# First transform stage of a long convolution: one full-height matmul on a 256-column block-diagonal table in place of two row tiles, under a new written-out order

## The chip, the core and the metric

The kernel runs on one core of a Trainium2 chip. A core has a matrix engine (TensorE, PE in the profile; its weight loads are listed as PEld), a vector engine (VectorE, DVE), an activation engine (ScalarE, ACT), a general one (GpSimd, POOL) and SyncE (SP), which here only issues DMAs. The engines run side by side, each through its own list of instructions, and wait for each other by semaphores. The metric is the device time of one execution in microseconds, the median of several runs.

## The reference, cut to what matters

The reference is one block of a network on 2048 tokens of 640 channels: an adaptive layer norm, a gated long convolution, another adaptive layer norm and a gated mixer.

```python
mod = (_silu(c) @ w_mod).reshape(1, 6, 1, -1)         # sa, ca, ga, sb, cb, gb
h = _layernorm(x) * (1 + ca) + sa
kv = short_conv4(A_k, shift_k) * A_v                  # 4 taps along the tokens
y = irfft(rfft(pad(kv)) * rfft(pad(ssm_k)))[:2048]    # causal convolution, length 4096
x = x + ga * h * (y + kv * ssm_D)
h = _layernorm(x) * (1 + cb) + sb
z = gelu(h @ w_in);  z1, z2 = halves(z);  z2 = _layernorm(z2)
out = x + gb * ((z1 * (w_sp @ z2 + b_sp)) @ w_out)
```

The convolution is computed by transforms written as matmuls. A sequence of 2048 tokens is cut in 16 pieces of 128, and a transform has two stages: stage 1 combines the 16 pieces of a channel, stage 2 works within the 128.

## The kernel before, in words

**Units.** The 640 channels are five units of 128. For each unit there is a filter transform (K, from ssm_k) and a data transform (U, from kv): ten stage-1 passes. An input tile X of a pass has the partitions (g, n), 8 channels by 16 pieces, and the free axes c (16 groups of 8 channels) and 128 tokens. So one slice X[:, c, :] holds the 16 pieces of 8 channels.

**Stage 1** (`stage1`, line 393). A pass has four steps (`s1`) of S1C = 4 slices c. In each step, for each slice, the lower and the upper 64 partitions are multiplied separately with a table of 128 columns, `F1flat[half]`: 32 frequencies j by 4 channels g, block-diagonal in g. These are two row tiles of TensorE, eight matmuls of 64 rows in a step. A step's result is 128 x 1024 fp32, two banks of PSUM (tag s1); in the first unit the two halves go to two single banks instead, tags pz and pu. A copy (`s1c`, on ACT, or on VectorE in some places) brings it to X1 in the order of frequencies.

**The table** (`f1_table`, line 283). VectorE makes angles (f1a) and a mask (f1g, `gmask`, from the bits of the partition number), ACT takes a cosine (f1c), VectorE multiplies (f1m).

**Stage 2** (`forward`, 8 items a pass): six matmuls of X1 with the sine tables M2, of 128 or 256 columns. For K, ACT copies the result (khc). For U, VectorE multiplies it with K's (prod, T at line 448), twelve matmuls with the tables G2 bring it back (inv), and a copy (zc) puts it in Z. Z is transposed by a DMA (zt) or, for the last unit, by TensorE (zfl); the last matmuls (y, yl) give y, which is multiplied with the normed and gated input gh.

**Beside it.** `short_conv`: taps on TensorE with diagonal weights dg, times V on VectorE (tv), written to memory (kvw) and read back as X of U. Layer norm statistics (ln1), the modulation vectors (modr, modc), the products ghm and sums res. Then the mixer: z in four groups of 512 tokens (zz and gelu), of which the first is transposed by TensorE and the others by DMA (turn), and the spatial matmul with the output projection (lines 912 to 940), which are scheduled apart.

**The order.** All but the last part is recorded as operations with their dependencies (class Plan), and then issued in one order written out by hand in the file: `ORDER` lists each operation with the engine that does it (P, A, D, G or S for SP). An engine works through its own operations strictly in that order. `FILLS` lists filler matmuls on the identity matrix, of 512 columns, which go to PSUM tag s1 and whose results nobody reads; they keep TensorE active.

Of the kernel before, what the change touches and what calls it, by code (L numbers as in the profile page):

```python
# [33 lines left out]
FILLS = (4, 4, 4, 2, 3, 1, 2, 4, 2, 1, 1, 3, 1, 2, )  # L34
# [5 lines left out]
D13 D95 D7 D9 D96 D97 D115 S14 D98 D109 A0 D110 A5 A4 A1 D103 A2 A3 G124 D8 A10 D116 A117 D104 A105 A106 A111 S77 D81  # L40
D11 P979 P980 P981 P982 P139 D6 A100 D12 P142 D144 A143 A140 D141 A99 G18 P983 P21 P19 A112 S78 D82 P145 P148 S16 D22
G101 S15 P25 G107 G108 G102 D20 S17 D26 P23 D24 P984 P130 G113 A118 D119 G120 S29 S467 A150 A147 A146 D131 A27 S28
A149 P151 A152 P155 A156 P133 S30 D134 P153 A154 A114 D121 P127 D31 A128 D471 P157 A158 D472 D473 P163 P985 P34 D35
A122 D123 G132 P165 A164 P161 A162 A166 S79 S80 P38 D39 P986 P167 D169 P170 P32 D33 A168 P136 A172 A171 G43 P176 D178
P173 D175 A174 G125 P36 D37 P159 A177 P179 S83 D85 D180 P987 P211 S468 A160 A137 S40 G129 P191 D192 A212 P988 P187
D188 S41 P213 A214 P181 D182 P203 G135 P217 A218 G138 P193 A194 P195 P215 A216 A475 A476 P189 D204 D196 D190 P183 S84
D184 G55 P199 D200 P205 A206 P44 S42 D474 D477 P185 A186 D478 D479 P223 A224 G480 P221 A222 S509 D45 P50 D51 P235 A236
P197 A198 P207 D208 P241 A242 P231 A232 P48 D49 P239 P46 A240 D481 D493 P225 A226 P237 A238 D47 P219 P510 A220 P512
A513 D497 S470 D486 A487 P243 D244 P201 A202 P255 P209 A494 S86 D88 P275 A276 P229 A230 D256 P251 P245 D488 D252 G67
P279 A210 A511 D498 A280 P247 D248 S469 S514 P227 A228 A246 D495 D496 P253 D254 P515 P267 D268 A499 D500 D516 S52 P277  # L50
P517 A278 A482 P257 D518 P233 A234 P263 D483 G558 D264 G614 P281 G616 A282 P249 S53 P58 G537 D484 A258 S87 P299 A300
P289 A290 P283 A284 P265 P303 A304 S54 P297 A298 P287 A288 D489 D485 D490 D59 P62 D63 P305 P271 D272 A306 A250 P60 D61
P301 A302 P293 A294 S519 P520 G491 P295 D521 G535 A296 D492 D505 A506 A266 P522 P307 A507 S89 D501 D502 A503 D308 G536
D91 G538 P273 S543 P315 D274 A508 P56 P269 D57 A270 A504 D523 G541 S65 P339 A340 P335 P309 A310 D316 P317 P259 D336
D260 P345 A346 P319 A318 P337 A338 P343 P285 G539 D540 D542 D320 A344 G556 D557 P544 D545 P261 A286 P331 D332 G593
G597 P341 A342 P291 A292 P321 P546 A262 D547 P351 P323 A352 G560 A322 S64 P72 P355 A356 P548 D324 P357 S66 D73 S90
P363 D549 A358 D651 A364 S92 D657 D561 P361 A362 G652 P550 D551 P327 D328 D94 P70 D71 P367 P347 A368 P68 P365 A366
G559 P311 D312 P325 P369 D618 D562 D563 G553 P74 S564 A348 P333 A370 A326 P371 A334 D69 D75 S76 S93 P403 P329 D372
A404 P565 D566 D599 P353 A354 A330 P379 D380 G595 P407 A408 P567 D568 P387 P313 P373 A314 G600 P349 A350 D388 A374
P569 D570 G554 P405 A406 P381 G598 D382 P571 D572 P359 G620 A360 P375 D376 P409 A410 G596 D583 P389 A390 P395 D396  # L60
P427 A428 D573 P411 A412 P377 P419 P399 D594 D587 D378 A420 G619 D400 P431 P397 D398 A432 P425 A426 P429 A430 P391
P401 D392 S601 P602 D603 A402 P383 P433 A434 P415 A416 D384 P604 D605 P393 A394 D586 P435 D436 P606 D607 P417 G658
P385 A418 G578 D582 P423 A386 A424 P451 D580 G617 P608 S698 P437 A438 D452 G552 D609 P421 A422 P443 D444 S524 P525
A526 G615 D655 P447 D448 P453 A454 P459 D460 P445 G613 A446 G656 G610 S622 G621 P455 D456 P449 A450 P463 D464 P461
A462 P413 A414 D574 P623 D624 P439 D440 D581 P457 G611 G588 S527 A458 P465 D577 A466 D653 P441 A442 P625 D576 P528
A529 S530 P663 A664 D612 D626 D579 D575 P627 D628 P659 D660 P989 P629 D630 P661 A662 P665 D666 D631 D632 D633 P990
P667 D668 D669 D672 D671 D670 P683 D700 D699 G654 G701 D684 P676 D677 D702 D703 D704 A126 P531 P690 D673 P533 A532
A534 P705 D706 P713 A714 D678 P711 D712 P991 P707 S697 D634 P709 D710 A708 P992 P741 D675 D635 D716 D674 P731 A742
G636 A732 D715 G717 D637 D638 D680 D782 D718 A719 D639 D720 P759 P738 P723 A724 D691 D685 P721 D679 A722 D781 A760
P734 P725 A726 P765 D681 D783 D640 D682 D784 G785 P727 D728 D786 D787 D789 D788 A735 P729 D641 D643 P763 D645 A730  # L70
D646 D642 G555 D688 A766 A790 P761 D585 P755 D592 A762 P773 A739 D649 A764 S791 D591 A756 D757 D647 P771 A772 P745
A746 D794 P767 A768 D793 D795 A774 P748 A749 P752 A796 P769 A770 A753 D792 P833 A834 D686 D589 P814 P825 A826 D644
D849 P797 A815 D590 P807 A808 D687 D848 D689 D584 D847 D850 G851 D852 D853 P821 D855 D854 A822 D692 D695 D816 D693
D696 D856 P800 A801 D694 D802 D915 A798 P827 A828 P811 D799 D648 D914 D747 D750 D751 D650 D916 A812 D813 D817 P831
A832 P804 A805 P837 A838 P818 A819 S857 D858 A862 D860 A861 P835 D913 P839 A840 P829 D859 P863 A830 G917 D806 A864
A836 D918 P884 D743 D809 P870 D919 D922 D920 A921 P901 A885 S923 A871 D872 D925 P895 A896 D926 P877 A902 P887 A888
D889 D928 P891 A892 D803 A878 D927 D736 P873 P866 A874 D875 A924 D754 A867 P899 A900 D740 D744 P880 A881 P929 P943
D758 A944 P932 A933 D820 A930 P893 A894 D823 D824 D810 G841 P946 A947 P936 A937 P959 D865 P961 P957 A960 A962 D842
D843 D845 A846 A844 P950 P967 D879 A968 D886 D733 D938 A951 P939 A940 D945 D868 P953 D737 D882 A954 G775 D776 A958
D890 A779 A778 P963 D869 D876 P905 D948 A964 D931 D883 G907 P903 A904 D908 D912 D934 D935 D949 A777 D911 P969 A906  # L80
P897 A898 D780 A910 D909 P965 D952 D955 D956 P971 A972 D941 D942 A970 G973 D974 A977 D975 D976 D978 A966
# [39 lines left out]
def kernel(  # L121
# [80 lines left out]
    with ExitStack() as actx:  # L202
# [3 lines left out]
        F1bd = consta.tile([P, NJ, 4], BF16)  # L206
# [16 lines left out]
        F1flat = F1bd[:].rearrange("p j g -> p (j g)")  # L223
# [27 lines left out]
        gmask, mpi, sgn = small("gmask", 4), small("mpi"), small("sgn")  # L251
        f1k, f1r, f1c = (consta.tile([P, NKC, 2], F32, name=n) for n in ("f1k", "f1r", "f1c"))
        f1i = consta.tile([P, NKC, 2], I32, name="f1i")
        bits = ((0, 15), (4, 3), (0, 3), (3, 15), (2, 1), (0, 1))
# [31 lines left out]
        def f1_table():  # L286
            def angles(e):
                e.scalar_tensor_tensor(f1i[:], f1k[:], pnum[:, 0:1], f1r[:], op0=ALU.mult, op1=ALU.add)
                e.tensor_scalar(f1i[:], f1i[:], 63, None, op0=ALU.bitwise_and)
            op("D", "f1a", angles, r=["bits0"], w=["f1a"])  # L290
            op("D", "f1g", lambda e: e.tensor_scalar(gmask[:], fidx[:, 0:4], pnum[:, 1:2], None, op0=ALU.is_equal),
               r=["bits0"], w=["f1g"])
            op("A", "f1c", lambda e: cosine(e, f1c[:], f1i[:]), r=["f1a", "sint"], w=["f1c"])
            op("D", "f1m", lambda e: e.tensor_tensor(
                F1bd[:], f1c[:].rearrange("p a b -> p (a b)")[:, :, None].to_broadcast([P, NJ, 4]),
                gmask[:, None, :].to_broadcast([P, NJ, 4]), op=ALU.mult), r=["f1c", "f1g"], w=["F1"])
# [96 lines left out]
        def stage1(u, X, X1):  # L393
            du = DU
            for ci, cp in enumerate(range(0, du // 8, S1C)):
# [5 lines left out]
                def mul(e, cp=cp, tiles=tiles, first=ci == 0):  # L401
                    if first:
                        new(X1, "X1", [P, NJ, DU])
                    ps = [new(*x, [P, 2 // len(tiles), S1C, NJ * 4], F32) for x in tiles]
                    for i in range(S1C):
                        for a in range(2):
                            half = slice(a * 64, a * 64 + 64)
                            mm((ps[a][:, 0] if pair else ps[0][:, a])[:, i, :], tl[X][half, cp + i, :], F1flat[half, :], True, True)

                def out_(e, cp, name, a0, na):  # L410
                    dst = tl[X1][:].rearrange("p j (a i g) -> p a j i g", a=2, g=4)[:, a0:a0 + na, :, cp:cp + S1C, :]
                    copy(e, dst, tl[name][:].rearrange("p a i (j g) -> p a j i g", g=4))
                op("P", "s1", mul, r=[(X, cp // 8 if pair else 0), "F1"] + ([(X1, "new")] if ci else []),
                   w=[x for x, _ in tiles] + ([] if ci else [(X1, "new")]), new=tiles + ([(X1, "X1")] if ci == 0 else []))
                na = 2 // len(tiles)
                for a, (x, _) in enumerate(tiles):
                    n1 = na * 128 * S1C
                    op("AD", "s1c", lambda e, cp=cp, x=x, a=a, na=na: out_(e, cp, x, a, na),
                       r=[x, (X1, "new")], w=[(X1, (cp, a))], n=n1)
# [567 lines left out]
```

## Time and profile before

| | |
|---|---|
| median of 13 runs | 339.95 us (338.14 to 342.63) |
| profiled execution | 340.28 us, its span 338.5 us |
| granted TensorE clock, mean | 0.99 |
| first matmul of stage 1 | 10.71 us |
| first matmul of the mixer | 149.24 us |
| busy: PE, DVE, ACT, POOL | 321.8, 219.6, 147.8, 72.0 us |
| stage-1 matmuls | 320 of 64 rows and 128 columns, in 40 steps |
| copies of 128 x 1024 after them on ACT | 32, mean 1.015 us |
| fillers | 34 matmuls of 512 columns |

The profile is one execution, seen by the hardware profiler. A line of a group or of the timeline names the line of the kernel, engine, operation, output and inputs, shapes, the count, the duration, and in brackets the idle time before it and what ended it. Line 237 is the helper of all matmuls in the first part and 240 that of all copies, so what they do is told by their tiles: s, pz and pu are PSUM tiles by tag, F1bd is the table of stage 1, X is the input or the result of stage 1, M and G are the sine tables, T is VectorE's product. Durations of TensorE overlap from one matmul to the next, so the cost of a group is taken from the start of the group to the start of the next.

### The profile page before, as it was taken

The numbers are of one execution on the slowest core, as the hardware profiler recorded it, in microseconds if no ns is written. First come the engines' busy times: TensorE is split into PE (matmuls) and PEld (weight loads), VectorE is DVE, ScalarE is ACT, GpSimd is POOL, SyncE is SP. The second block draws the span as 40 slices with busy tenths as digits, with TensorE's granted clock in tenths as the row PEclk, the third lists the DMA queues.
The fourth block names the chain that finished last, engine by engine and source line by source line (L and its number), as shares of the span: only waits on it lengthen the run. The fifth ranks groups of instructions, "written<-read, shape, count | busy, mean of one in ns | idle before, by whom it ended". The sixth has DMA issues, their size and how long they took to land.

```text
span 338.5 us, 6933 instructions
## 1 busy us (share of the span) xinstructions
PE 321.8 (95%) x2887; PEld 208.5 (62%) x2887; DVE 219.6 (65%) x460; ACT 147.8 (44%) x251; POOL 72.0 (21%) x88
## 2 busy tenths in 40 slices
PE   7789999998999899989999999999999999999995
PEld 2365868767768699845455555555555555555553
DVE  7699998989898999998685676253322232223323
ACT  2666889897667664538667579100000000000000
POOL 2561030568048606132001022000000000000000
PEclk9799999999999999979999999999999999999999
DMA  8989998999494938601442992165555566621421
GB/s 130 196 158 238 214 285 205 183 254 224 79 159 116 270 99 190 229 2 26 54 77 40 173 222 88 39 140 110 122 124 118 116 136 134 108 62 46 48 46 58
DMA packets 128582, 45.02 MB, mean 133 GB/s; under 512 B 117704, under 2 KB 127784, under 8 KB 128552
## 3 DMA queue, kind: packets, MB, share of 16 engines
q1 hardware_dynamic: 126448, 44.32, 62.5%
q10 hardware_dynamic: 2104, 0.27, 0.5%
q8 instruction: 22, 0.36, 0.4%
q14 instruction: 8, 0.07, 0.1%
HBM read 16.11 MB, written 5.24 MB: 63 GB/s over the span
## 4 chain that ended last, share of the span: by engine, by line
PE 53%; DMA 2%; DVE 1%; issue 0%; DVEq 0%
PE ps L919 28%; PE po L937 9%; PE pz L237 8%; PE pu L237 8%; DMA Z<-Z 2%; DVE Z L834 0%; PE sm L798 0%; PE s L237 0%; DVE u L922 0%; DVE ot L939 0%; DVE Z L807 0%; PE pt L929 0%; DVE Z L786 0%; DVE xt L661 0%; DVEq L834 0%
## 5 line engine op out<-in xcount | busy, mean ns | idle before, releaser
L919 PE MATMUL ps<-X,wT 128*128 128x432 bf16 x512 | 95.7, 346 | 0.0
L919 PEld LDWEIGHTS <-wT 128*128 128x128 bf16 x512 | 50.1, 98 | 42.2
L930 ACT COPY uT<-pt 128x896 bf16<-128x896 bf16 x1 | 0.9, 906 | 117.0 <-PE pt L929 117.0
L448 DVE TENSOR_TENSOR T<-pu,KH 128x1024 bf16<-128x1024 f32 x40 | 48.3, 1217 | 3.4 <-PE pu L237 1.6
L237 PEld LDWEIGHTS <-Z 128*128 128x128 bf16 x320 | 31.4, 99 | 28.4 <-issue 1.1
L237 PE MATMUL pu<-X,M 128*128 128x128 bf16 (+1 forms) x480 | 45.8, 237 | 2.4 <-DVE T L448 2.3
L237 PE MATMUL pz<-T,G 128*128 128x128 bf16 (+1 forms) x480 | 41.5, 237 | 0.8 <-DVE T L448 0.8
L237 PEld LDWEIGHTS <-M 128*128 128x128 bf16 x480 | 35.7, 98 | 8.6 <-issue 3.4
L922 DVE SCALAR_TENSOR_TENSOR u<-ps,bcol,G 128x432 bf16<-128x432 f32 x18 | 12.0, 667 | 42.2 <-PE ps L919 42.2
L237 PEld LDWEIGHTS <-G 128*128 128x128 bf16 x480 | 34.8, 98 | 4.6 <-DVE T L448 1.0
L240 ACT CAST X<-s 128x1024 bf16<-128x1024 f32 x32 | 32.5, 1015 | 11.1 <-PE s L237 11.1
L237 PE MATMUL pz<-big,Z 128*128 128x432 bf16 x160 | 33.1, 352 | 0.0
L937 PE MATMUL po<-w_o,uT 128*128 128x320 bf16 (+1 forms) x224 | 32.8, 299 | 0.0
L237 PE MATMUL pu<-big,Z 128*128 128x432 bf16 x160 | 32.0, 346 | 0.5 <-DVE Z L834 0.5
L937 PEld LDWEIGHTS <-uT 128*128 128x128 bf16 (+1 forms) x224 | 21.8, 98 | 9.8
L922 DVE SCALAR_TENSOR_TENSOR u<-ps,bcol,M 128x432 bf16<-128x432 f32 x14 | 9.3, 667 | 28.3 <-PE ps L919 28.3
L240 ACT CAST KH<-pu 128x512 bf16<-128x512 f32 x40 | 23.1, 592 | 8.1 <-PE pu L237 7.9
L939 DVE TENSOR_TENSOR ot<-po,xt 128x320 bf16<-128x320 f32 x32 | 15.7, 491 | 13.4 <-PE po L937 13.4
L240 ACT CAST Z<-pz 128x512 bf16<-128x512 f32 x33 | 19.2, 589 | 8.9 <-PE pz L237 8.9
L237 PE MATMUL sm<-big,dg 128*128 128x512 bf16 (+1 forms) x80 | 21.2, 393 | 1.0 <-DVE dg L503 1.0
L624 POOL TENSOR_TENSOR gh<-gh,gsa_bf 128x512 bf16<-128x512 bf16 x14 | 16.7, 1205 | 18.5 <-DVE gh L624 16.7
L863 DVE BATCH_NORM_STATS2 stz<-X 128x6 f32<-128x432 bf16 x32 | 17.7, 586 | 1.6 <-ACT X L857 1.6
(139 smaller groups left out, 371.1 us busy)
## 6 DMA issues: line engine op xcount, KB each, us to landing
wm<-in_w_mod_dram SPq DMA_DIRECT2D x6, 800.0 KB, 5.7
xt<-in_A_q_dram SPq DMA_DIRECT2D x4, 640.0 KB, 5.8
out_dram<-ot SPq DMA_DIRECT2D x16, 160.0 KB, 2.4
big<-in_B_w_in_dram SPq DMA_DIRECT2D x2, 1080.0 KB, 7.2
X<-in_A_ssm_k_dram SPq DMA_DIRECT2D x4, 512.0 KB, 7.3
kv_scr<-big SPq DMA_DIRECT2D x4, 512.0 KB, 3.4
X<-kv_scr SPq DMA_DIRECT2D x4, 512.0 KB, 5.7
w_o<-in_B_w_out_dram SPq DMA_DIRECT2D x6, 160.0 KB, 2.9
```

What stands on the lines that cost most here:

```text
L237: nc.tensor.matmul(o, lhsT=w, rhs=x, start=start, stop=stop)
L240: (e.copy if e is nc.scalar else e.tensor_copy)(dst, src)
L448: e.tensor_tensor(T_[:], tl[pu][:, :, :, None, :].to_broadcast([P, KP, 2, 2, DU]), tl[KH][:, :, None, :, :].to_broadcast([P, KP, 2, 2, DU] ...
L624: lambda e, vec=vec, o=o: e.tensor_tensor(gvu, gvu, vec[:, None, d0:d0 + du].to_broadcast([P, TB, du]), op=o),
L863: op("D", "stz", lambda e, i=i, n=n, fc=fc: e.bn_stats(out=stz[:, n, fc, :], in_=tl[z2][:, i, fc * FC:(fc + 1) * FC]), r=[(z2, (i, fc))], ...
L919: nc.tensor.matmul(ps[:, :FC], lhsT=wTs[t][:, s_, :], rhs=tl["z2_%d" % (s_ // TB)][:, s_ % TB, fc * FC:(fc + 1) * FC], start=(s_ == 0), st ...
L922: nc.vector.scalar_tensor_tensor(u[:, sl], ps[:, :FC], bcol[:, t:t + 1], z1[t][:, sl], op0=ALU.add, op1=ALU.mult)
L930: nc.scalar.copy(uTs[t][:], pt[:])
L937: nc.tensor.matmul(ps[:, :HS], lhsT=uTs[t][:fsz[ft], ft, :], rhs=w_o[:fsz[ft], ft, h * HS:(h + 1) * HS], start=(ft == 0), stop=(ft == NFT ...
L939: nc.vector.tensor_tensor(ot[:, h * HS:(h + 1) * HS], ps[:, :HS], xt[:, t, h * HS:(h + 1) * HS], op=ALU.add)
```

## The change

The table gets twice the columns: for every partition now (a, j, g), with a the lower or upper half of the eight channels, and the mask has eight columns instead of four, compared with three bits of the partition number instead of two. So one matmul of 128 rows and 256 columns gives for a slice what the two half-height matmuls gave together. A step has four matmuls instead of eight. The result of a slice now lies together, (a, j, g), and a bank holds two slices of both halves instead of four slices of one half; the copy to X1 reads it accordingly. In the first unit the two single banks hold two slices each. The total of copied elements stays.

The small loads of c, D and the taps may be given to GpSimd too, but stand where they were, on ACT. The order of all operations is new, with other engines for some of them, and twelve fillers of together 22 matmuls instead of fourteen of 34.

```diff
-FILLS = (4, 4, 4, 2, 3, 1, 2, 4, 2, 1, 1, 3, 1, 2, )
+FILLS = (4, 4, 4, 1, 2, 1, 1, 1, 3, 1, 2, 2, )
 ORDER = """
-D13 D95 D7 D9 D96 D97 D115 S14 D98 D109 A0 D110 A5 A4 A1 D103 A2 A3 G124 D8 A10 D116 A117 D104 A105 A106 A111 S77 D81
-D11 P979 P980 P981 P982 P139 D6 A100 D12 P142 D144 A143 A140 D141 A99 G18 P983 P21 P19 A112 S78 D82 P145 P148 S16 D22
+D13 D95 D12 D96 S14 D97 D103 D109 D104 D110 A0 D115 A5 A4 A1 A2 A3 A111 D98 A99 D6 D18 P979 P980 P981 P19 S16 A112 P21
+D7 D8 D9 S77 D81 S78 A10 D11 G124 G125 D20 P139 A106 D82 D141 P142 A105 A140 A144 P982 P145 A146 D22 G31 D143 D116
...
-        F1bd = consta.tile([P, NJ, 4], BF16)
+        F1bd = consta.tile([P, 2, NJ, 4], BF16)
...
-        bits = ((0, 15), (4, 3), (0, 3), (3, 15), (2, 1), (0, 1))
+        bits = ((0, 15), (4, 7), (0, 3), (3, 15), (2, 1), (0, 1))
...
             op("D", "f1m", lambda e: e.tensor_tensor(
-                F1bd[:], f1c[:].rearrange("p a b -> p (a b)")[:, :, None].to_broadcast([P, NJ, 4]),
-                gmask[:, None, :].to_broadcast([P, NJ, 4]), op=ALU.mult), r=["f1c", "f1g"], w=["F1"])
+                F1bd[:], f1c[:].rearrange("p a b -> p (a b)")[:, None, :, None].to_broadcast([P, 2, NJ, 4]),
+                gmask[:].rearrange("p (a g) -> p a g", a=2)[:, :, None, :].to_broadcast([P, 2, NJ, 4]), op=ALU.mult), r=["f1c", "f1g"], w=["F1"])
...
-                    ps = [new(*x, [P, 2 // len(tiles), S1C, NJ * 4], F32) for x in tiles]
+                    k = S1C // len(tiles)
+                    ps = [new(*x, [P, k, 2 * NJ * 4], F32) for x in tiles]
                     for i in range(S1C):
-                        for a in range(2):
-                            half = slice(a * 64, a * 64 + 64)
-                            mm((ps[a][:, 0] if pair else ps[0][:, a])[:, i, :], tl[X][half, cp + i, :], F1flat[half, :], True, True)
+                        mm(ps[i // k][:, i % k, :], tl[X][:, cp + i, :], F1flat, True, True)
...
-                    dst = tl[X1][:].rearrange("p j (a i g) -> p a j i g", a=2, g=4)[:, a0:a0 + na, :, cp:cp + S1C, :]
-                    copy(e, dst, tl[name][:].rearrange("p a i (j g) -> p a j i g", g=4))
+                    dst = tl[X1][:].rearrange("p j (a i g) -> p a j i g", a=2, g=4)[:, :, :, i0:i0 + k, :]
+                    copy(e, dst, tl[name][:].rearrange("p i (a j g) -> p a j i g", a=2, g=4))
...
-        op("SA", "ldc", lambda e: e.dma_start(c_bf[:], c[0].rearrange("(t p) -> p t", p=P)), w=["c"])
+        op("SAG", "ldc", lambda e: e.dma_start(c_bf[:], c[0].rearrange("(t p) -> p t", p=P)), w=["c"])
```

In the new order, among other moves: the first two tap groups of the short convolution (P19, P21) stand ahead of the first stage-1 step (P139), and their diagonal weights are made by VectorE (D18) ahead of the table's angles; the first half of V (S16) is loaded ahead of the first X (S77, S78); both writes of the first kv are issued by SP; the two halves of w_in are loaded earlier, ahead of the last K input; the preload of the gelu table (A126) stands near the end.

## The prediction

> **What bounds the kernel now.** I read the page's busy line and slices first, then the stages, then TensorE's timeline at single transform steps. Busy time, and the slices of 8.5 us:
>
> ```profile
> PE 321.8 (95%) x2887; PEld 208.5 (62%) x2887; DVE 219.6 (65%) x460; ACT 147.8 (44%) x251; POOL 72.0 (21%) x88
> PE   7789999998999899989999999999999999999995
> DVE  7699998989898999998685676253322232223323
> PEclk9799999999999999979999999999999999999999
> ```
>
> TensorE is nearly always occupied; VectorE nearly as much in the first 18 slices, and not after. The clock row dips twice. By stages (time, then busy us of PE, PEld, DVE, ACT, POOL, then clock):
>
> ```profile
> 0.00:11.00 11.00, 6.39 (x25) 2.15 (x27) 7.40 (x31) 3.92 (x10) 2.22 (x15) 1.00 0.94 141
> 11.00:50.00 39.00, 37.32 (x417) 24.97 (x411) 34.45 (x65) 28.12 (x50) 14.87 (x17) 0.96 1.02 222
> 50.00:100.00 50.00, 48.28 (x621) 37.65 (x620) 46.01 (x79) 41.49 (x65) 21.68 (x19) 1.00 0.97 184
> 100.00:149.00 49.00, 44.84 (x769) 39.47 (x764) 46.10 (x73) 28.24 (x45) 22.78 (x21) 0.99 0.60 162
> ```
>
> The mixer starts at 149.24 us; from there PE is busy 185 of 189 us with work the diff doesn't edit. So the 149 us in front decide. There PE is busy 136.8 us, VectorE 134.0: PE bounds, with VectorE 3 us behind. The chain of waits reaches back only to 146 us and can't say what set the front.
>
> One transform step on PE (start, duration, work, count):
>
> ```profile
> 41.24 1.05 PE L237 MATMUL pz<-T,G 128*128 128x256 bf16 x12
> 42.12 1.05 PE L237 MATMUL pu<-X,M 128*128 128x256 bf16 x12
> 43.01 1.03 PE L237 MATMUL sm<-big,dg 128*128 128x512 bf16 x4
> ...
> 45.19 0.60 PE L237 MATMUL pu<-X,M 128*128 128x256 bf16 x6
> 45.73 0.40 PE L237 MATMUL s<-F1bd,X 64*128 64x128 bf16 x8
> 46.06 0.61 PE L237 MATMUL pu<-X,M 128*128 128x256 bf16 x6
> 46.51 0.81 PE L237 MATMUL sm<-big,dg 128*128 128x512 bf16 x3
> ```
>
> Durations overlap, so starts are subtracted. Twelve pu matmuls take 43.01 - 42.12 = 0.89 us, six therefore 0.445; ahead of a stage-1 step the six take 45.73 - 45.19 = 0.54. So 0.095 us is lost in entering. The eight half-height matmuls then take 46.06 - 45.73 = 0.33 although their four pairs run at 0.056 each (pairs start at 15.45, 15.50, 15.56, 15.62 in the first unit), 0.22 together: 0.10 is lost in leaving. A step alone costs 0.425, of which 0.195 is switching.
>
> The start, where PE waits for the table:
>
> ```profile
> 10.29 0.20 DVE L389 TENSOR_TENSOR X<-X,D_col 128x8 bf16<-128x8 bf16 x1 [1.57 <-issue]
> 10.37 0.29 DVE L294 TENSOR_TENSOR F1bd<-f1c,gmask 128x128 bf16<-128x128 f32 x1
> ...
> 10.71 0.21 PE L237 MATMUL pz<-F1bd,X 64*128 64x128 bf16 x1 [2.19 <-DVE F1bd L294]
> ...
> 11.42 1.46 PE L237 MATMUL s<-ident 128*128 128x512 bf16 x3
> ```
>
> Until 10.71 us PE has done only filler. That wait is followed by a window at half clock, 11.05 to 14.46 us.
>
> [...] 3.41 us windows at 0.5, one after the table wait, one at 147.58 to 151.0; 512-column matmuls start 0.425 us apart there, 0.216 elsewhere. [...]
>
> **The change, part by part.**
>
> 1. Stage-1 matmuls. 40 steps of eight 64-row, 128-column matmuls become four 128-row, 256-column ones. Price of a 256-column matmul: twelve pz (four of 256, eight of 128) take 42.12 - 41.24 = 0.88; eight of 128 at 0.056 are 0.448; so 0.108 each. New step: 4 x 0.108 = 0.432, total 17.3 us. Old: 40 x 0.224 = 9.0, plus switching. In the order the 40 steps stand in 36 separate groups, 36 x 0.195 = 7.0; total 16.0. **+1.3 us of PE.** [...]
>
> 2. Fillers: 34 matmuls become 22, 12 x 0.216 = 2.6 us of PE. They fill gaps in which PE has nothing ready, so leaving them out is no gain by itself: I count zero here. That the new order has fewer such gaps to fill is worth something, at most 2.6 us; see (8).
>
> 3. The start. The first two tap groups of the short convolution now precede the first stage-1 step. They need dg (now built by VectorE ahead of the F1 angles) and the first K half. VectorE runs three of the four turn and msub pairs first; by its old timeline that ends about 7.6 us, then the sk cast 0.1 and dg 0.6: ready about 8.4 us. The K half has landed by 5.3 (the D load, which waits for it, starts at 5.34). F1bd still waits for D_col, as before at 10.29; its multiply doubles to 256 elements, 0.29 to an estimated 0.4; f1c stands behind three sines of 0.4 and is ready about 9.8, hidden by D_col. X's loads move behind one V transpose on SP (2.48 us issue) and should land 2 to 3 us later, still about when D_col does. So eight taps of 0.216, **1.7 us of real work, are done in a gap where PE had nothing.** **-1.7 us.** If PE's work from 8.4 to 10.1 also keeps the clock up, another 0 to 1.7 is saved; I take 0[...].
>
> 4. Copies out of PSUM: ACT's 128x1024 at 1.01 us as before, but the four innermost steps now alternate between two banks. No row shows that[...]. ACT has 149 - 102 = 47 us idle in front, so I take 0 on the path.
>
> 5. Moves between engines ahead of the mixer, counted in the two orders: VectorE gets +3 xn (0.44 each by start differences), +1 s1c (1.2), +1 zc (0.61), +1 gcopy (0.65), +1 zk (0.6), +2 gneg[...], +2 ln2, less one ghm, msgn, res and yml: **+4.4 us of VectorE, -7 of ACT.** VectorE has 15 us idle in front, so nothing on the path by itself; it is the cover that rival R1 takes away.
>
> 6. DMA queues. kv0's second write and first write both go on SP (one was ACT's); V0 moves ahead of X; w_in's halves of 1080 KB move ahead of the fifth K load and the last two Z transposes. w_in was loaded at 112.8 and 137.0 and is needed after 148[...]. Behind it on SP stand XK4 and ZT1. Landing takes 7.2 for the one and 5.6 for the other, 12.8 if the second waits for the first; SP can issue both once U3's load is out, and by the order's PE work (summed from the starts) K4's first step comes 12 us after that. No wait there before; bound 0 to 2 us, I take 0.3.
>
> 7. The mixer's beginning. Before, the second token group's transpose was issued 10 us in and PE waited:
>
> ```profile
> 158.53 3.02 SPq L826 DMA_TRANSPOSE Z<-Z  x1
> ...
> 165.94 1.09 PE L237 MATMUL pu<-big,Z 128*128 128x432 bf16 x5 [0.51 <-DVE Z L834]
> ```
>
> In the new order the transpose is emitted 6.9 us of PE work after the first mixer matmul instead of 9.7, while that group's first matmul stays at 15.1. The wait of 0.7 us (the start is 0.68 late) should go: **-0.7.** What is late next is the z2 normalisation, which shows no wait. The gelu table load (1.28 us) is no longer preloaded, but falls between the last modulation and the first gelu, while PE has a filler and a matmul group of 0.9; four PSUM buffers cover the rest: 0.
>
> 8. Fewer gaps. I credit 0.8 of the 2.6 in (2), since most measured stalls (0.8 to 1.7 us at 78, 84, 115, 138, 145) were queueing that fillers don't mark.
>
> Sum: +1.3 - 1.7 + 0.3 - 0.7 - 0.8 = -1.6 us. The profiled execution took 340.28 us (span 338.5 and 1.8 around it): 338.7. The median of 13 is 0.33 lower: **338.3.**
>
> **Rivals.** (R1) *VectorE becomes the bound, slower.* Up to the first stage-1 step of the last unit's K transform, summed start differences give VectorE about 88 us against PE's 87, where before it was 82 against 87. Products release each inverse matmul. Against: after that point VectorE has less to do than before. It decides once VectorE's idle in front, 15 us less 4.4, is less than what its waits for PE use; those waits were 8 us (2.9, 1.9, 1.6, 0.6, 0.5 and 0.4 in the list of waits). If two thirds of 4.4 us turn into PE waits, +2.9: 338.3 + 2.9 = 341.2; all of it, 342.7.
>
> (R2) *The gain at the start is hidden.* Stage 2 needs the M2 sines, signs and negations; if they arrive as before (first pu<-X,M at 18.34), PE idles for the taps' 1.7 us there. Then 338.3 + 1.7 = 340.0. Against: the new order has all four sign ops on POOL and three sines ahead of f1c.
>
> (R3) *It works better.* The clock dip at 11 us goes (-1.7) and idle time shrinks by another 0.6: 336.0. For it: [...] the fewer fillers.
>
> (R4) *The change doesn't do what it says*: the 0.195 is no mode switch but part of any change of tile, and stays: +7, 345.3. Against: pz to pu at 42.12 shows no such loss.
>
> **Chances.** Sum above 0.43; R3 0.17; R2 0.19; R1 0.19; R4 0.02. A measurement can tell about 0.3%, 1.0 us, from no change. The main case and R3 are faster, R2 within, R1 and R4 slower: 0.60, 0.19, 0.21. Range: the main case alone 337.0 to 339.3; to leave out no more than 2 in 10 it takes in most of R3 and R1: 335.6 to 341.6.
>
> **What would show it.** Stage-1 steps of four matmuls at 0.43 with no 0.1 us ahead or behind; taps at about 8.5 us, before the first F1bd matmul near 10.8; first pu<-X,M near 16.5; mixer's first matmul at 148.0 to 148.6 and no wait at the first transposed group; VectorE 138 us busy in front. Wrong if the mixer begins after 149.2, or PE's waits for T (3.1 us before) exceed 5.

## The result, and the profile after

| | before | after |
|---|---|---|
| median | 340.25 us (338.07 to 342.63, 48 runs) | 336.89 us (336.62 to 337.36, 11 runs) |
| ratio of the two | | 0.991, 95% interval 0.9889 to 0.9931 |
| profiled execution, its span | 340.28, 338.5 us | 337.21, 335.3 us |
| first stage-1 matmul | 10.71 us | 11.81 us |
| first forward transform (pu<-X,M) | 18.34 us | 18.07 us |
| U0's first stage-1 step | 26.61 us | 25.52 us |
| first inverse transform (pz<-T,G) | 34.20 us | 31.25 us |
| mixer's first matmul | 149.24 us | 145.79 us |
| from there to the spatial matmul (ps) | 60.51 us | 60.81 us |

The change makes the kernel faster by 0.9%, 3.4 us; 338.3 was forecast. All of it is there when the mixer begins, and 2.95 of the 3.45 us already at the first inverse transform. Of these 2.95 about 0.9 is only moved: six pu matmuls and one stage-1 step that stood ahead of that point now stand behind it. The times of the table also contain the half-clock windows of the two profiled executions: at 11.05 to 14.46 and 147.58 to 151.0 us before, at 140.8 to 144.2 after.

The page of the changed kernel, busy line and slices:

```profile
PE 321.2 (96%) x2719; PEld 214.3 (64%) x2719; DVE 222.7 (66%) x468; ACT 140.3 (42%) x242; POOL 72.7 (22%) x89
PE   6799999999989999999999999999999999999995
DVE  7988999899999999997885775263222332223323
PEclk9999999999999999889999999999999999999999
```

TensorE's busy sum has not changed, though 160 of the 320 stage-1 matmuls and eight fillers are gone: the new matmuls have twice the columns. The clock's dip in the second slice is gone; one is left at 140.8 to 144.2 us. The same stages as before:

```profile
0.00:11.00 11.00, 7.44 (x20) 2.23 (x20) 8.62 (x31) 3.31 (x9) 3.54 (x16) 1.00 1.00 136
11.00:50.00 39.00, 36.50 (x358) 27.87 (x359) 36.00 (x75) 30.21 (x54) 11.74 (x14) 1.00 1.02 236
50.00:100.00 50.00, 48.28 (x560) 40.61 (x558) 46.97 (x77) 36.42 (x59) 26.89 (x24) 1.00 0.92 206
100.00:149.00 49.00, 47.89 (x729) 41.00 (x726) 46.87 (x79) 26.83 (x43) 20.92 (x21) 0.97 0.54 129
```

VectorE is busy 138.5 us in the first 149, 134.0 before; but 3.2 us of the mixer lie in these 149 us now. Up to the mixer's first matmul it is busy 135.3 us, 134.2 before. A transform step on TensorE (start, duration, work, count):

```profile
32.13 0.60 PE L237 MATMUL pu<-X,M 128*128 128x256 bf16 x6
32.57 0.60 PE L237 MATMUL s<-F1bd,X 128*128 128x256 bf16 x4
33.01 1.05 PE L237 MATMUL pz<-T,G 128*128 128x256 bf16 x12
```

Six pu take 0.44, four stage-1 matmuls 0.44, and nothing is lost at either end. The start, on TensorE:

```profile
8.55 1.90 PE L237 MATMUL sm<-big,dg 128*128 128x512 bf16 x8 [0.64 <-DVE dg L502]
11.81 0.38 PE L237 MATMUL pz<-F1bd,X 128*128 128x256 bf16 x2 [1.36 <-DVE F1bd L294]
...
17.41 0.61 PE L359 MATMUL sm<-ident,M 128*128 128x128 bf16 x8 [1.24 <-POOL M L342]
...
18.07 1.05 PE L237 MATMUL pu<-X,M 128*128 128x256 bf16 x12
...
25.52 0.39 PE L237 MATMUL pz<-F1bd,X 128*128 128x256 bf16 x2 [0.36 <-DMA X<-kv_scr]
...
31.25 1.04 PE L237 MATMUL pz<-T,G 128*128 128x256 bf16 x12
```

The taps run at 8.55 at full clock, but the table comes 1.1 us later than before, and a new wait for the M2 signs stands ahead of the first forward transform. Then the mixer's beginning, first TensorE, then GpSimd and VectorE on the way to the first of these waits:

```profile
149.70 0.40 PE L797 MATMUL sm<-ident,Z 128*128 128x128 bf16 x4 [0.72 <-DVE Z L785]
156.42 1.07 PE L237 MATMUL pz<-big,Z 128*128 128x432 bf16 x5 [0.51 <-ACT M L856]
```

```profile
147.16 1.16 POOL L660 TENSOR_TENSOR xt<-xt,gh 128x512 bf16<-128x512 bf16 x1
147.23 1.10 DVE L773 SCALAR_TENSOR_TENSOR nmr<-mv,rstd 128x2 f32<-128x2 f32 x1
```

The wait for the transposed group (0.51 before) is gone; two others took its place.

**The clock as a second measure.** A window of 3.41 us at half clock lowers a run's mean clock by about 1.7 / 338 = 0.005, so a run's mean clock tells roughly how many such windows it had (in the profiled executions two and 0.990 before, one and 0.995 after). Of 100 runs of the kernel before beside the experiments, 11 had a mean of 0.998 or more (median 338.62), 31 had 0.993 to 0.997 (340.13) and 58 had 0.991 or less (340.62). Of the changed kernel's twelve runs whose clock was recorded, eight had 0.998 or more (336.75) and four 0.993 to 0.997 (337.15). So with the clock up in both the difference is 1.9 us; the other 1.5 us of the 3.4 go with windows at half clock, which the changed kernel has less often.

### The profile page after: what moved, and what is told of

Its sections match the earlier page's. It is cut to its first block, busy times and chain, and to the rows that moved or that the text cites. A ratio compares the mean times of both kernels' runs of the same rounds, so it can differ in the third digit from the quotient of the medians.

```text
span 335.3 us, 6591 instructions
## 1 busy us (share of the span) xinstructions
PE 321.2 (96%) x2719; PEld 214.3 (64%) x2719; DVE 222.7 (66%) x468; ACT 140.3 (42%) x242; POOL 72.7 (22%) x89
## 4 chain that ended last, share of the span: by engine, by line
PE 73%; DVE 16%; DMA 5%; issue 2%; POOL 1%; ACT 0%; DVEq 0%; SPq 0%; ACTq 0%
PE ps L918 28%; PE pz L237 15%; PE pu L237 14%; PE po L936 9%; DVE T L447 5%; PE sm L237 5%; PE s L237 2%; DVE big L517 2%; DMA D_col<-in_A_ssm_D_dram 2%; DMA X<-kv_scr 1%; DMA big<-in_A_k_dram 1%; DVE X L240 1%; DVE gh L623 1%; DVE st L666 1%; POOL rstd L183 1%
## 5 line engine op out<-in xcount | busy, mean ns | idle before, releaser
L237 PEld LDWEIGHTS <-Z 128*128 128x128 bf16 x320 | 31.1, 98 | 27.7 <-issue 1.1
L237 PE MATMUL pu<-X,M 128*128 128x128 bf16 (+1 forms) x480 | 45.4, 237 | 0.8 <-DVE T L447 0.7
L237 PE MATMUL pz<-T,G 128*128 128x128 bf16 (+1 forms) x480 | 41.2, 237 | 0.7 <-DVE T L447 0.6
L237 PEld LDWEIGHTS <-M 128*128 128x128 bf16 x480 | 37.1, 98 | 6.3 <-issue 1.3
L237 PEld LDWEIGHTS <-G 128*128 128x128 bf16 x480 | 35.3, 98 | 3.6 <-DVE T L447 0.8
L240 ACT CAST X<-s 128x1024 bf16<-128x1024 f32 x31 | 31.5, 1015 | 11.2 <-PE s L237 11.0
L237 PE MATMUL pz<-big,Z 128*128 128x432 bf16 x160 | 32.3, 346 | 0.5 <-ACT M L856 0.5
L237 PE MATMUL pu<-big,Z 128*128 128x432 bf16 x160 | 32.5, 346 | 0.1
L237 PE MATMUL sm<-big,dg 128*128 128x512 bf16 (+1 forms) x80 | 20.4, 379 | 1.1 <-DVE dg L502 0.6
L623 POOL TENSOR_TENSOR gh<-gh,gca_bf 128x512 bf16<-128x512 bf16 x14 | 16.8, 1205 | 16.9 <-DVE gca_bf L610 12.9
```

The costliest lines, as they stand in the source:

```text
L237: nc.tensor.matmul(o, lhsT=w, rhs=x, start=start, stop=stop)
L240: (e.copy if e is nc.scalar else e.tensor_copy)(dst, src)
L623: lambda e, vec=vec, o=o: e.tensor_tensor(gvu, gvu, vec[:, None, d0:d0 + du].to_broadcast([P, TB, du]), op=o),
```

## Experiments

In kernels with another order the code lines are shifted by six (L231 for L237). Times are medians; the ratio is to the kernel before.

**1. Shape and order apart.** The change couples a new matmul shape with a new order. Shape alone:

```diff
 # the changed kernel
-ORDER, FILLS = new
+ORDER, FILLS = those of the kernel before
```

> The order and the fillers of before, with the full-height stage-1 matmuls and their table alone. Theory A (the gain is in the order[...]): +0 to +1.3 us on before, 340.2 to 341.6. Rival B (the shape is what gains[...]): 337 to 338.5, most of the way to the changed kernel.

Measured 341.55 us (14 runs), 1.0022 [1.0004, 1.0041]. The full-height matmuls cost 1.2 us, as the forecast's step 1 had it (1.3). They don't gain anything by themselves.

Order alone, with the old row tiles:

```diff
 # the kernel before
-ORDER, FILLS = old
+ORDER, FILLS = those of the changed kernel
```

> The changed kernel's order and fillers, with the two row tiles of before. Theory A: the whole gain of the order without the 1.3 us that the full height costs, 335.5 to 337.0. Rival B: 339 to 341. A third outcome, 337.0 to 338.5, would say that the order has absorbed the difference and the shape doesn't matter to the time.

Measured 337.60 us (6 runs), 0.9913 [0.9891, 0.9935]: 0.7 slower than the changed kernel, not 1.3 faster: the third outcome of the expectation. Its mixer begins 1.28 us earlier (144.51; about 0.4 of this is the half-clock window just ahead of the changed kernel's mixer: experiment 9's profiled run, without one at a mean clock of 1.000, has the first transpose there at 143.00, the changed kernel at 143.42), but the way from there to the spatial matmul takes 62.4 us instead of 60.8. So under the new order what TensorE saves in front comes back as waits in the mixer. The list of waits of this kernel from 143 to 207 us (what waited, for whom, us in total, times, longest):

```profile
PE sm L792 <- DVE Z L780: 0.9, 1, 0.9
PE pz L231 <- ACT M L851: 0.5, 1, 0.5
PE pu L231 <- ACT Z L826: 0.4, 2, 0.2
PE pu L231 <- DVE Z L828: 0.4, 1, 0.4
PE sm L792 <- DVE Z L801: 0.2, 1, 0.2
```

The changed kernel has only the first two of them, 0.7 and 0.5.

**2. Start and rest of the order apart**, both with full height, cut at the first inverse transform.

```diff
-ORDER = new
+ORDER = new up to the first inverse, then the old order of what is left
```

> Full height. Up to the first inverse matmul the changed kernel's order and fillers, all other operations after that in the order of before. Theory A1 (of the 3.45 us that the mixer starts earlier in the profiles, 2.95 are there when the first inverse matmul starts): 337.0 to 338.5. Rival A2 (the order gains all along the first 145 us, and the early lead would be lost in a wait later): 339.5 to 341.

```diff
-ORDER = new
+ORDER = old up to the first inverse, then the new order of what is left
```

> Full height. Up to the first inverse matmul the order and fillers of before, the rest in the changed kernel's order. A1: most of the gain is gone, 339.3 to 341.3. A2: most of it stays, 337.0 to 338.5.

New start: 337.96 us (6 runs), 0.9931 [0.9906, 0.9957]. Old start: 341.55 us (22 runs), 1.0034 [1.0013, 1.0055], a little above A1's range. The start carries the gain: 341.55 (all old) less 337.96 is 3.6 us. The new rest behind an old start is worth nothing in the medians, behind the new start another 1.1 us (337.96 to 336.89).

Windows at half clock are only a part of this. Behind the new rest the start is worth 4.7 us in the medians (341.55 to 336.89), and still 3.0 with runs of a mean clock of 0.998 or more alone (339.8, 8 runs; 336.75, 8). The profiled execution with the old start had no such window in its first 330 us (mean clock 0.998), and shows where these 3.0 come from:

```profile
10.68 0.38 PE L231 MATMUL pz<-F1bd,X 128*128 128x256 bf16 x2 [3.15 <-DVE F1bd L288]
...
17.19 1.05 PE L231 MATMUL pu<-X,M 128*128 128x256 bf16 x12
...
25.80 0.39 PE L231 MATMUL pz<-F1bd,X 128*128 128x256 bf16 x2 [0.27 <-DMA X<-kv_scr]
...
34.05 1.05 PE L231 MATMUL pz<-T,G 128*128 128x256 bf16 x12
```

The changed kernel has these at 11.81, 18.07, 25.52 and 31.25. So with the clock up the new start is 0.9 us later at the first forward transform, level at U0's first stage-1 step, where both wait for the kv that is read back (0.27 and 0.36), and 2.8 us ahead at the first inverse, 0.9 of them the moved work. From the first forward transform to the first inverse, TensorE spends 4.6 us on fillers and idling behind the old start and 1.8 behind the new one (16.86 us less 12.3 of work; 13.18 less 11.4; the work counted by the starts, with 0.88 for twelve pu, 0.44 for four stage-1 matmuls and for eight of the L353 or L359 kind, 0.216 for a tap).

**3. What in the start?** The first tap groups put back behind the first two stage-1 steps, as in the old order:

```diff
-... P19 S16 A112 P21 ... D20 P139 A106 D82 D141 P142 A105 A140 A144 P982 ...
+... S16 A112 ... P139 A106 D82 D141 P142 A105 A140 A144 P19 P21 D20 P982 ...
```

> The changed kernel with the first two tap groups put back behind the first two stage-1 steps on TensorE, and the first product of the taps (VectorE) with them. Nothing else is edited, the dg block stays early. Theory T (my step 3: 1.7 us of real work is done in a gap): the median rises by 1.2 to 1.9 us, to 338.1 to 338.8, and both the first kv write and U0's first stage-1 step come later by about as much. Rival R2 (the gain was hidden, since the first forward transform waits for the M2 signs at 17.41 anyway, with 1.24 us of idle before it): the first forward transform stays within 0.4 of 18.07 and the median within 0.4 of 336.9.

Measured 340.95 us (22 runs), 1.0007 [0.9988, 1.0026]: the whole gain is gone with the place of these eight matmuls, over twice what theory T expected. TensorE in it:

```profile
11.61 0.59 PE L231 MATMUL pz<-F1bd,X 128*128 128x256 bf16 x2 [3.86 <-DVE F1bd L288]
...
13.27 3.62 PE L231 MATMUL sm<-big,dg 128*128 128x512 bf16 x8
...
22.15 1.05 PE L231 MATMUL pu<-X,M 128*128 128x256 bf16 x12
```

The wait for the table is 3.86 us, and what follows until 17.5 runs at half clock (the clock row has 0.6 in the slice of 8.5 to 17.0 us): the taps take 3.62 us, 1.90 in the changed kernel. The first forward transform comes 4.1 us later, U0's first stage-1 step 4.2, the mixer 3.8. From the lengths of the matmuls in this stretch of 5.9 us (columns at half clock less columns at full clock) 2.9 us are lost there to the clock; if all of that reaches the end, the other 1.1 to 1.2 is the order. The split isn't exact: two of these runs had a mean clock of 0.995, and at 339.95 are still 2.8 above the changed kernel's runs at that clock. Rival R2 as written here is out; even the 1.24 us wait for the signs did not absorb the taps.

**4. Is it the reading back of kv?** In the old order a V transpose stood on SyncE's queue ahead of U0's loads of X. With full height:

```diff
-... S28 ... S30 ... S79 S80 ...
+... S28 ... S79 S80 S30 ...
```

> Old order and old fillers with full-height matmuls (as e1_full_old), and on SyncE's queue the two loads of X from kv_scr are issued ahead of the V transpose that stood before them (3.9 us of queue time in the kernel before). Theory K (the gain of the new start lies in the kv write and read-back being earlier): these loads are issued near 19.0 instead of 23.1, U0's first stage-1 step starts by 24.7 instead of 26.0 (the four fillers ahead of it hide the rest), and the median falls by 0.6 to 1.3 us against e1_full_old: 0.998 to 1.000 of the kernel before. Rival P (what counts is that PE has taps to do in the gaps, the loads are not what it waits for): the loads come earlier but the median stays within 0.4 us of e1_full_old, 1.001 to 1.0035 of the kernel before, or gets worse because the V transpose now comes late for its taps.

Measured 342.30 us (8 runs), 1.0063 [1.0033, 1.0094], slower than experiment 1. SyncE's queue, then TensorE:

```profile
19.25 0.34 SPq L517 DMA_DIRECT2D kv_scr<-big  x1
22.51 0.99 SPq L373 DMA_DIRECT2D X<-kv_scr  x2
23.56 2.69 SPq L479 DMA_TRANSPOSE big<-in_A_v_dram  x1
```

```profile
29.21 1.02 PE L231 MATMUL sm<-big,dg 128*128 128x512 bf16 x4 [1.00 <-DVE big L511]
```

The loads wait until 22.51 for the write issued at 19.25: the write held them now, not the queue (in the changed kernel the write issued at 17.98 lands 2.61 us later, and the loads go at 20.64). And V is now late for its taps. The size of the loss is not the edit's alone, since these runs had a low mean clock, 0.984 to 0.990. The loads did not come near 19.0 as theory K had it, so this run doesn't settle what earlier loads are worth. In the changed kernel they are issued at 20.64 us, 23.15 before: the second kv write is 0.6 us earlier (17.98, 18.59) and the transpose behind it takes 1.88 us instead of 3.91. But the old start with its clock up (experiment 2) issues them as early, at 20.35.

**5. The late D load.** ScalarE issues the load of D_col at 5.42 us, when the first K half has landed, and its table load and the sines stand behind it. GpSimd has cleared D_col by 2.33 us, so that is not what it waits for: in the chain of the changed kernel it stands behind the transfer of this K half, issued at 0.72 and landed 4.62 us later. Why it waits for that, no trace shows. Here D_col is cleared first on GpSimd instead of last:

```diff
+        nc.gpsimd.memset(D_col[:], 0.0)
         nc.gpsimd.iota(pint[:], [[0, 1]], base=0, channel_multiplier=1)
...
-        nc.gpsimd.memset(D_col[:], 0.0)
```

> The changed kernel with one line moved: GpSimd clears D_col first, before its six index tables, instead of last. Nothing else is edited. In the changed kernel the load of D_col is issued by ScalarE at 5.42 us, when the first K half has landed, and ScalarE's first table load (6.79) and the sines stand behind it. Here [...] it should be issued at about 1.8 us. Theory D (the start is bounded by this late load): D_col lands by about 6, the table load begins near 3.2 instead of 6.8, F1bd's first matmul comes at about 11.2 instead of 11.81 (VectorE's own work ends there), the first forward transform (pu<-X,M) at 16.5 to 17.5 instead of 18.07, and the median falls by 0.4 to 1.2 us against the changed kernel: 335.7 to 336.5. Rival S (a later chain, the write of kv and its reading back, sets the start): the milestones move by the same amounts but U0's first stage-1 step stays at 25.5 +- 0.3, and the median stays within 0.3 of the changed kernel's 336.9.

Measured 337.05 us (6 runs), 0.9918 [0.9887, 0.9949], the same as the changed kernel. The load is issued at 1.78; then on ScalarE:

```profile
2.99 1.28 ACT L707 ACT_TABLE_LOAD   x1 [2.99 <-POOL mbase L271]
...
7.07 0.51 ACT L338 ACTIVATE M<-T,mturn 128x256 bf16<-128x256 f32 x1 [2.36 <-DVE T L335]
```

The table load moved up by 3.8 us, and ScalarE idles 2.4 us for VectorE. One cause is gone, the next holds at nearly the same place. The median lies within rival S's 0.3 us, not in theory D's range. The milestones of neither are met in the profiled execution: it had a half-clock window at the taps (the eight take 3.25 us), behind a wait of 1.80 us, and is later throughout (U0 at 26.26).

**6. VectorE's order in the start as well.**

```diff
-D13 D95 D12 D96 D97 D103 D109 D104 D110 D115 D98 D6 D18 D7 D8 D9 D81 D11 ...
+D13 D95 D7 D8 D9 D12 D96 D97 D98 D109 D110 D6 D18 D81 D11 D103 D104 D115 ...
```

(D7 to D9 the F1 angles and mask, D97 to D115 the turns and subtractions of M2, D18 dg, D11 F1bd; the D load first as in 5, and f1c first on ScalarE.)

> As e7_D_first (D_col cleared first), and VectorE's order in the first 11 us changed so that it no longer holds up what has become ready: the F1 angles go ahead of the turns, only two of the four turn and subtract pairs (not three and a half) stand ahead of dg, and F1bd's multiply goes ahead of the other turns; ScalarE makes f1c first. In e7_D_first the D load came 3.6 us earlier and ScalarE then idled 2.4 us for VectorE, and the median did not move. Theory V (VectorE's order is what bounds the start after the D load): the taps begin at 7.6 to 8.2 instead of 9.0 and F1bd's first matmul at 9.5 to 10.3 instead of 12.08, the first forward transform at 15.8 to 17.2 instead of 18.7, U0's first stage-1 step is at least 0.8 earlier than 25.5, and the median is 335.4 to 336.4. Rival L (loads bound it: the second half of X, the second K and V blocks, then the kv write and read-back): the taps and F1bd come earlier but U0's first stage-1 step stays at 25.5 +- 0.4 and the median within 0.4 of 336.9.

Measured 336.76 us (5 runs), 0.9895 [0.9864, 0.9926]. Its range (336.25 to 336.83) and the changed kernel's overlap, so this is no shown improvement. All five runs had a mean clock of 0.998 or more, and the changed kernel's at that clock take as long (336.75). TensorE:

```profile
10.31 0.38 PE L231 MATMUL pz<-F1bd,X 128*128 128x256 bf16 x2
...
12.49 0.38 PE L231 MATMUL pz<-F1bd,X 128*128 128x256 bf16 x2 [0.92 <-ACT X L234]
...
17.11 0.61 PE L354 MATMUL sm<-ident,M 128*128 128x128 bf16 x8 [1.15 <-POOL M L337]
```

F1bd's first matmul comes 1.5 us earlier than in the changed kernel and with no wait after the taps. Then a wait for a copy and the one for the signs take 1.2 of it back: the first forward transform is 0.3 earlier. U0's first step comes at 25.02, 0.5 earlier, and the mixer begins 0.93 earlier (144.86; about 0.4 of it the window ahead of the changed kernel's mixer), of which the median shows 0.1. That is rival L in the median; U0 moved a little more than it allowed.

**7. The next wait too.** M2 chunks 0 and 1, which alone the first forward transform needs, made first on all three engines, and the E angles behind the second kv's products:

```diff
-D97 D98 D109 D110 D6 D18 D81 D11 D103 D104 D115 D20 D82 D141 D22 D143 D116 D121 D26 D24 D128
+D97 D98 D103 D104 D6 D18 D81 D11 D109 D110 D82 D20 D141 D22 D143 D115 D116 D26 D24 D128 D121
```

> As e12_start_vec, with what showed up as late next in its trace moved too: the M2 chunks 0 and 1, which alone the first forward transform needs, are made first on VectorE, ScalarE and GpSimd (in e12_start_vec one sine of chunk 0 ran at 13.4, though its input was ready at 6.5, and the signs followed at 14.0 to 17.1), the second D addition goes ahead of the last two chunks, and the E angles (1.9 us of VectorE) go behind the two products of the second kv block. Theory C (the start is a chain of such waits, each hidden by the one before it, and is worth time until the loads end it): the 1.15 us wait for M at 17.11 goes, the first forward transform starts at 16.2 to 17.0 instead of 17.77, the second kv write is issued at 16.2 to 17.0 instead of 17.68, U0's first stage-1 step at 23.5 to 24.5 instead of 25.02, and the median is 335.2 to 336.2. Rival B (what is won in the start is lost again before the mixer or in it, as the 0.9 us that e12_start_vec's mixer began earlier, of which the median showed 0.1): the milestones come earlier as said, and the median stays at 336.4 to 337.0.

Measured 337.26 us (6 runs), 0.991 [0.9895, 0.9926]: 0.4 to 0.5 slower than 6. The wait for the signs is gone, but:

```profile
12.88 0.39 PE L231 MATMUL pz<-F1bd,X 128*128 128x256 bf16 x2 [1.01 <-DVE X L384]
14.05 0.38 PE L231 MATMUL pu<-F1bd,X 128*128 128x256 bf16 x2 [0.78 <-DVE X L234]
```

Two waits for VectorE's addition and copy came instead, and in the profiled execution (the longest of the six, 339.29 us) a half-clock window behind them (four taps at 14.92 take 1.91 us, 1.03 in experiment 6); its milestones are therefore no measure for the others. Both theories expected earlier milestones; neither is met. In experiments 5 to 7 every wait of TensorE from 8 to 15 us is for VectorE or ScalarE.

**8. Fillers.** Those after the first three groups issue nothing:

```diff
-FILLS = (4, 4, 4, 1, 2, 1, 1, 1, 3, 1, 2, 2)
+FILLS = (4, 4, 4, 0, 0, 0, 0, 0, 0, 0, 0, 0)
```

> The changed kernel without its fillers, but for the three groups of four before the first stage-1 step: the other nine groups (10 matmuls on the identity, 2.2 us at 0.216 each) issue nothing. What is computed is the same. Theory Z (my step 2: fillers stand in gaps in which TensorE has nothing ready, so they cost and bring nothing): within 0.3 us of the changed kernel's 336.9. Rival F (fillers hold TensorE up when its work is ready): 1 to 2 us faster, 335 to 336. Rival C (fillers keep the clock granted): slower by 1 us or more, by more windows at half clock, 338 and above.

Measured 337.17 us (6 runs), 0.9909 [0.9881, 0.9938]: theory Z. (These groups hold 14 matmuls, not the ten of the expectation: 3.0 us.) Their mean clock is 0.985 to 0.995, the changed kernel's 0.995 to 1.0: without fillers there are more windows at half clock, but the medians show no loss by them. In the profiled run, with a mean clock of 0.994, the window lies at 139.8 to 143.2 us, and TensorE waits 0.40 and 0.54 right behind it; where the others had theirs is not recorded.

**9. The gelu table loaded early again.**

```diff
-... D704 P705 ... D975 A126 P961 ...
+... D704 A126 P705 ... D975 P961 ...
```

> The changed kernel with one operation moved: ScalarE loads the gelu table early again (before the second gb copy, as the kernel before did) instead of at the first gelu (146.0 to 147.3). Theory G (the missing preload causes the new wait in the mixer's beginning): the first gelu begins at about 146.4 instead of 147.3, the wait of 0.51 at 156.42 shrinks to under 0.2, and the median falls by 0.3 to 0.6 us. Rival N (the wait comes from the normalisation of the second token group, whose copies stand ahead of the gelus on ScalarE): the first gelu is earlier but the wait near 156.4 keeps 0.4 or more and the median stays within 0.25 us.

Measured 337.48 us (7 runs), 0.9935 [0.9907, 0.9963]: not faster but 0.6 slower. ScalarE:

```profile
142.21 1.28 ACT L726 ACT_TABLE_LOAD   x1
...
144.79 0.56 ACT L798 ACTIVATE Z<-sm,sb_col,cb_col 128x256 bf16<-128x256 bf16 x1 [0.77 <-ACT gb_bf L610]
```

The load takes the same 1.28 us but stands ahead of the second gb copy, and the modulation that feeds the mixer waits for it. The gelus don't come sooner (147.24, 147.33 in the changed kernel), and the wait for M near 156 is 0.5 as before. The same with the old row tiles:

```diff
 # new order, row tiles (as in experiment 1)
-... D704 P705 ... D975 A126 P961 ...
+... D704 A126 P705 ... D975 P961 ...
```

> New order and new fillers with the old half-height row tiles (as e2_tiles_new), and the gelu table loaded early. e2_tiles_new began its mixer 1.28 us before the changed kernel and lost 1.6 us in it by waits at 147.2, 154.3, 161.4 and 162.2. Theory G: the early table takes 1.0 or more of these waits away, and the median is 336.2 to 336.8, below the changed kernel's 336.9. Rival N: the waits are those of the normalisation and of the transposes, which start from the end of the output transform's work on VectorE and GpSimd; the median stays at 337.3 to 337.8.

Measured 338.08 us (20 runs), 0.9943 [0.9929, 0.9958], 0.5 slower than without it. Theory G falls both times. Rival N has the wait right, but both times are above its ranges: leaving the preload out is worth about 0.5 us.

## Why the prediction was near, and where it failed

The sum was -1.6 us; measured were -3.4, of which 1.9 with the clock up in both. The sign, the shape's price and the new order as the cause of the gain were right. The clock was a term put at nothing, step 3 did not come about in the way described, step 7 failed, and step 8 was put too small. That -1.6 and -1.9 lie so close is luck: errors of either sign make up for each other.

1. *Stage-1 matmuls, +1.3*: right. 0.44 a step, no loss at its ends, +1.2 by experiment 1. R4, the switching not being one, is out.
2. *Fillers, 0*: right (experiment 8). They were miscounted, here and in the description of the change: 34 became 26, not 22 (the page has 168 matmuls fewer, 160 of stage 1 and eight), so 1.7 us of them went, not 2.6.
3. *The start, -1.7, with "another 0 to 1.7" for the clock of which 0 was taken*: the taps do run in the gap, but two things were missed. The first is the clock. With the taps late 5.9 us at half clock follow the wait for the table and cost 2.9; the changed kernel's runs have few windows and those before have more, 1.5 us by the grouped medians. That was R3's first term and should have been in the main case: the row of the clock showed the window right behind the wait that the taps were to fill. The 0 was my estimate. In the profiled execution, with the taps from 8.55 to 10.4, the clock was up until 140.8 us; in experiment 5's, with its taps at 9.04, a window came all the same. What decides between the two was not shown. The second is that with the clock up the taps' gain is not seen at the first forward transform: 18.07 us, where 16.5 was forecast and the old start has 17.19. F1bd was late (11.81, 10.8 forecast): an instruction of VectorE's angles took 0.99 us, to the end of GpSimd's dg (below), and 0.25 in the kernel before. Then the signs were waited for, 1.24 us. So R2 was right up to that point. What the early taps win there within the new order, 1.1 us by experiment 3's split, the later table and the signs take back. The time is won behind it, by fewer fillers and waits up to the first inverse transform, 1.8 us instead of 4.6.
4. *Copies, 0*: right. Median 1.01 us before and after.
5. *Moves between engines, 0*: right for the path, and R1 is out: TensorE's waits for T are 1.3 us, 3.1 before. The count of +4.4 us for VectorE is not what the trace shows: up to the mixer it is 1.1 us busier (135.3, 134.2), in the whole run 3.1.
6. *Queues, +0.3*: no wait for the fifth K input is in TensorE's list. Not tested apart.
7. *The mixer's beginning, -0.7*: this step failed. The named wait is gone, but "what is late next ... shows no wait" did not hold: 0.72 and 0.51 came instead. With the full height and the new rest, the way from the mixer's start to the spatial matmul is 60.8 to 60.9 us, in the changed kernel and in the profiled runs of experiment 2 (old start), 5 and 6; with the old rest it is 60.05 and 60.06 (experiment 2, new start, and experiment 1). So it is about 0.8 longer, not 0.7 shorter. The 60.51 of the kernel before contain part of a half-clock window: its first five matmuls there take 1.78 us, such five take 0.91 elsewhere. Leaving out the gelu preload, put at 0, was a gain of about 0.5 (experiment 9).
8. *Fewer gaps, -0.8*: too small. This is where most of the gain with the clock up is: 2.8 us fewer fillers and waits behind the first forward transform (experiment 2). The new rest brings the mixer forward by another 1.4 us (147.22 with the new start and the old rest, 145.79 here, with a window at half clock just ahead) and gives 0.8 of it back within the mixer.

What stays open: which of the start's moves take away the fillers and waits from 18 to 31 us, and why the new rest is worth 1.1 us behind the new start and nothing behind the old.

## What to carry to other kernels

Two waits of TensorE here (2.19 us before, 3.86 in experiment 3) had half clock behind them, and time was lost twice, in the wait and to the clock (1.7 and 2.9 us): there, work that is put into the gap can be worth more than its own length (eight taps of 1.90 us made 4.1 us of the median in experiment 3). It need not: with the old start and the full height, waits of 3.0 and 3.15 us at the same place had no window behind them in the profiled runs. So read the clock row first, and compare the milestones of two executions only where their clocks agree: here the kernel before had a window in its start, and only the old start without one shows that the first forward transform did not come earlier. Where several engines are near their limit in one stretch, as in the first 15 us here, taking one wait away shows the next: three edits (experiments 5 to 7) that each took away the wait they were made for changed the median by 0.1 to 0.4 us. And a new shape is best judged apart from the order written for it: here shape alone lost, order alone gained.

## What the runs showed of the hardware that was not expected

A short instruction of VectorE lasted here, at two places, until a GpSimd instruction beside it ended. The F1 angle took 0.25 us in experiment 6, where GpSimd was idle; in the changed kernel it took 0.99, until GpSimd's dg ended:

```profile
9.27 1.04 POOL L502 TENSOR_TENSOR dg<-ident,sk 128x512 bf16<-128x512 bf16 x1
9.36 0.99 DVE L288 SCALAR_TENSOR_TENSOR f1i<-f1k,pnum,f1r 128x32 int32<-128x32 f32 x1
```

9.36 + 0.99 = 10.35, and 9.27 + 1.04 = 10.31. The same stands behind the wait in the mixer's beginning: the tiny nmr starts 0.07 us after GpSimd's sum and ends with it. Of the mixer's five such operations two run beside that sum before (1.10 and 0.75 us) and three after (1.09 to 1.11), each to within 0.02 us of its end; with GpSimd idle they take 0.16. Why they last so long, no trace shows. So the next thing to try is to keep GpSimd's sum off nmr's place; that was not tried.

The half-clock windows also go with groups among the runs of one kernel (338.62, 340.13 and 340.62 us above): the kernel before spreads over 4.6 us, the changed one over 0.7.
